# Second layer of a two-layer MLP kernel: block products by seven in a fourth group, sums by accumulating transfers, and x blocks placed earlier

## The chip, the cores and the metric

The kernel runs on one core of one Trainium2 chip. The metric is the time of one execution on the device in microseconds (us). The core's engines are called as in the profile: PE multiplies matrices, PEld loads its weights, DVE and ACT work on vectors, POOL is the general engine, and SP issues most of the DMAs. PE reads SBUF and writes sums to PSUM; DVE and ACT carry them from there to SBUF.

## The reference

An attention without softmax gives x (4608 tokens, 512 columns), and two layers follow. All data are float32.

```python
kv = np.einsum('bhsd,bhse->bhde', k, v)
out = np.einsum('bhsd,bhde->bhse', q, kv)          # then scaled by its rms and g_norm
# layer 1:  h = x @ w_in;  g = relu(h) ** 2;   x = g @ w_out      (w_in 512 x 2048, w_out 2048 x 512)
# layer 2:  h = x @ w_in;  g = h * cos(h);   out = g @ w_out
```

## The kernel before

**Products in three parts.** Each float32 operand is split into a high part in PE's reduced float32 format (a copy on ACT, names ending in `h`) and a low part (a subtraction on DVE, names ending in `l`). A product is three matmuls: high by high, high by low, low by high.

**The stages.** The attention and one half of layer 1's hidden units run first, in 72 chunks (`run_chunks`, to about 501 us). While they run, the weights are converted: `load_w` and `conv_steps` read a piece of raw weights, split it and store it in DRAM, as `wi_d` (first products), `ws_d` (second products by seven) or `wo_d` (plain second products). Items of the kind "seven" cost four more DVE differences, and more ACT and DVE splitting, than items of the kind "out". After that come 30 slots (`run_slots`): 10 for the rest of layer 1 (five tiles of tokens with two groups of hidden units each), and 20 for layer 2 (five tiles with four groups). Four tiles have 1024 tokens and the last one has 512. In this text a slot is named by its number from 0 to 29; slots 10 to 13 are the four groups of layer 2's first tile, and 26 to 29 those of its last tile.

**A slot.** The first product (`first_product`, line 502) is done as a product of 2 x 2 blocks with seven block products instead of eight (the Winograd form), which is 84 matmuls. Its two PSUM tiles FA and FB take turns, and between the block products ACT and DVE read them (`keep`, `add`, `last`). Then the activation runs, in layer 2 the five steps `cos_1` to `cos_5` for each of four blocks, three on ACT and two on DVE. The second product of the slot follows 1.25 slots after its first product (`LAG2`), and its matmuls are interleaved with the first product of the next slot. It has two forms. In the set `seven` (line 82) it is done by seven block products as well (`second_product`, line 675): `s_block` makes four differences on DVE and seven splits (ACT and DVE), and in layer 2 a full tile takes 168 matmuls of 256 columns. Each of the seven sums is carried by `drain_product` from PSUM (tiles SA and SB, in turn) into one of four running sums in SBUF, by a DVE addition (line 698), or by an ACT copy (line 695) where the running sum begins. Groups that are not in `seven` go the plain way (`second`, line 604, then `drain`): four splits (`g_hi`, `g_lo`), 96 matmuls of 512 columns in a full tile, and eight DVE additions of half size (line 624).

**Order and queues.** Each step has a place in units of a slot, given with `at(pos(...))`; `PH` is a seventh of a slot. Instructions of one engine run in order. SP issues the weight loads `wi` (line 476), `ws` (481) and `wo` (486) of 512 KB each, the loads of a tile's x (`load_quads`, line 442), and the results (`later`, line 842): the DMA of a result waits on SP until its last addition has been made, and the loads behind it wait as well. Weights and running sums share 16 buffers (`w_p`), the x blocks 13 (`x`), and the activation's tiles 18 (`c`). `x_block` (lines 452, 470, 471) makes the seven blocks of a tile's x, 11 DVE instructions and 7 on ACT, at -1.9 to 4.1 sevenths of a slot from the tile's first slot; `load_quads` stands at -3.6 and -2.6 sevenths.

Of the kernel before, what the change touches and what calls it, by code (L numbers as in the profile page):

```python
# [8 lines left out]
F32 = mybir.dt.float32  # L9
# [7 lines left out]
P = 128  # L17
# [5 lines left out]
def kernel(  # L23
# [55 lines left out]
    wi_d = {  # L79
        (m, q): dram.tile([P, NPR, 2, 2, 2, P], F32, name=f"wi_d{m}_{q}") for m in range(2) for q in groups_of[m]  # L80
    }
    seven = {(0, 0)} | {(1, q) for q in range(NP - 1)}
    ws_d = {k: dram.tile([P, NPR, 2, 2, 2, P], F32, name=f"ws_d{k[0]}_{k[1]}") for k in sorted(seven)}
    wo_d = {
        (m, f): dram.tile([P, 2, DM], F32, name=f"wo_d{m}_{f}")
# [338 lines left out]
    W_OF = (0, 1, 3, 4, 6, 5, 2)  # L424
    BLOCKS = {(0, 0): 2, (1, 1): 5, (0, 1): 6, (1, 0): 7}
    S_ORDER = (0, 2, 3, 4, 5, 1, 6)
    xb, wi, wo, kept, hs, ys, sums, quads = {}, {}, {}, {}, {}, {}, {}, {}

    def big(pool, dtype, name, ht):
# [157 lines left out]
    def second(k, n):  # L587
        m, t, q = slots[k]
        ht = TILES[t][1]
        todo = units(k)[4 * n:4 * n + 4]  # L590
        for a, c in enumerate(CHUNKS):
            pp, u = divmod(c, 2)
            w = wo[k, c]
            for b, (j, i) in enumerate(todo):
                ps = psum["SA" if b < 2 else "SB"][:, b % 2, :512 if m else ht]
                g = gs[k, (u, j)]
                cs = slice(i * P, (i + 1) * P)
                for x, y in ((0, 0), (0, 1), (1, 0)):
                    if m == 0:
                        lhs, rhs = w[:, x, cs], g[y][:, pp, :]  # L600
                    else:
                        lhs, rhs = g[y][:, pp, cs], w[:, x, :]
                    last = a == 3 and (x, y) == (1, 0)
                    nc.tensor.matmul(  # L604
                        ps, lhs, rhs, start=(a == 0 and (x, y) == (0, 0)), stop=last, skip_group_check=True
                    )
                    if last and b % 2:
                        drain(k, 2 * n + b // 2)
                    yield

    def drain(k, n):
        m, t, q = slots[k]
        t0, ht = TILES[t]
        j, i = units(k)[2 * n]
        ps = psum[("SA", "SB")[n % 2]]
        if m == 0:
            e, ps = sums[m, t, i // 2, j][:, :, :ht], ps[:, :, :ht]
            nc.vector.tensor_tensor(out=e, in0=ps, in1=e, op=ALU.add)
            if q == groups_of[m][-1]:
                later(0.1, nc.sync.dma_start, out=y_d[t][:, j, i:i + 2, :], in_=e)  # L620
            return
        for d in range(2):
            e = blocks_of(t, sums[m, t, d, j])[:, i:i + 2, :]
            nc.vector.tensor_tensor(out=e, in0=ps[:, :, 2 * P * d:2 * P * (d + 1)], in1=e, op=ALU.add)
            if i + 2 == ht // P:
                dst = out[t0 + j * ht:t0 + (j + 1) * ht, 2 * P * d:2 * P * (d + 1)]
                later(0.1, nc.sync.dma_start, out=dst.rearrange("(b p) n -> p b n", p=P), in_=blocks_of(t, sums[m, t, d, j]))

    def s_block(k, i):
        m, t, q = slots[k]  # L630
# [23 lines left out]
    def blocks_of(t, x, m=1):  # L654
        if m == 0:
            return x[:, :, :TILES[t][1]]
        return x.rearrange("p c n -> p (c n)").rearrange("p (b n) -> p b n", n=2 * P)[:, :TILES[t][1] // P]
# [32 lines left out]
    def drain_product(k, i):  # L690
        m, t, q = slots[k]
        ps, (d, j) = blocks_of(t, s_bank(k, i), m), SUM_OF[i]
        if q == 0 and m and i in (0, 2, 3, 6):
            sums[m, t, d, j] = e = w_p.tile([P, 2, 512], F32, tag="w", name="sum")
            nc.scalar.copy(out=blocks_of(t, e), in_=ps)
        else:
            e = blocks_of(t, sums[m, t, d, j], m)
            nc.vector.tensor_tensor(out=e, in0=ps, in1=e, op=ALU.add)


    chunks = [(t, f) for t in range(NTILE) for f in range(NH)]
# [5 lines left out]
    def at(n, fn, *a):  # L707
        jobs.append((n, len(jobs), fn, a))
# [25 lines left out]
    def outs_of(m, ps):  # L734
        return [("out", m, f, 1) for p in ps for f in (2 * p, 2 * p + 1)]

    def pairs_in(m, ps, kind="pair"):
        return [(kind, m, p, i) for p in ps for i in range(2)]
# [4 lines left out]
        w_items += new  # L743
        w_at += [n + step * k for k in range(len(new))]
    for new, n0, n1 in (
        (pairs_in(0, range(4, 6), "seven") + outs_of(0, range(6, 8)) + outs_of(1, range(6, 8)) + pairs_in(1, range(4), "seven"), 13, nAtt + 1),
        (pairs_in(0, range(NP, 2 * NP)), nAtt + 1, nA0 - 6),
        (pairs_in(1, range(2 * NP)) + pairs_in(1, range(4, 6), "seven"), pos(0.5), pos(9)),
    ):
        w_items += new  # L750
        w_at += [n0 + (n1 - n0) / len(new) * k for k in range(len(new))]
# [24 lines left out]


    PH = 1 / 7
    for k, (m, t, q) in enumerate(slots):
        if q == 0:  # L780
            for a in range(2):
                at(pos(k + (a - 3.6) * PH) if k else nA0 - 6, load_quads, m, t, a)
            for f, i in enumerate(ORDER):
                at(pos(k + (f - 1.9) * PH) if k or f > 2 else nA0 - 4 + f, x_block, k, i)
        for f, i in enumerate(ORDER):
            at(pos(k + (f - 2.7) * PH) if k or f > 2 else nA0 - 5 + f / 2, load_wi, k, i)
        if (m, q) in seven:
# [48 lines left out]
    def later(delay, fn, **a):  # L836
        pending.append((here + delay, fn, a))
# [118 lines left out]
```

## Time and profile before

| what | us |
|---|---|
| median of 3 runs (lowest, highest) | 1594.78 (1592.71, 1594.97) |
| the profiled execution, its own time | 1593.87 |
| its span in the trace | 1592.1 |
| PE busy | 1555.1 |
| DVE busy | 1273.3 |
| ACT busy | 992.7 |

The granted clock of PE over the span is 0.994 of full speed. 1.8 us of the execution's time lie outside the span. In the rows further down, times in a window or in a timeline are us from the span's start. A row of the windows view lists for a stretch each engine's busy time with the number of its instructions, then the granted clock, the mean busy share of the 16 DMA engines and the rate.

### The profile page before, as it was taken

What the parts mean: (1) busy time and instruction counts of PE and PEld (TensorE: products, weight loads), DVE (VectorE), ACT (ScalarE), POOL (GpSimd) and SP (SyncE); (2) the same over time, 40 slices, a digit from 0 to 9 for tenths busy, and PEclk for the clock granted to TensorE, in tenths of its full rate; (3) what the DMA queues carried; (4) which work ended last, traced back from release to release, by engine and by line L of the source; (5) the groups of instructions that cost most, each with busy time, mean ns of one, the idle gap of its engine ahead of it and who ended that gap; (6) DMA issues with size and microseconds to landing.
All of it is one profiled execution on the core that took longest, in us unless ns stands there. A gap on an engine that the chain in (4) does not pass through costs nothing.

```text
span 1592.1 us, 23679 instructions
## 1 busy us (share of the span) xinstructions
PE 1555.1 (98%) x8840; PEld 1322.0 (83%) x8840; DVE 1273.3 (80%) x1724; ACT 992.7 (62%) x1422; POOL 60.8 (4%) x58
## 2 busy tenths in 40 slices
PE   5999999999999999999999999999999999999998
PEld 4777777778887778888888899889988998899897
DVE  7967767787766898989867789868986898689786
ACT  5977767784434666556646666666666666666664
POOL 1100112111100000000000000000000000000000
PEclk8999999999999999999999999999999999999999
DMA  9855876665568989898988856565656565656684
GB/s 316 279 168 159 256 238 223 200 207 184 164 214 274 318 283 352 304 353 292 351 311 333 286 177 212 180 244 172 212 187 237 172 213 180 229 174 206 214 338 191
DMA packets 214545, 382.20 MB, mean 240 GB/s; under 512 B 17312, under 2 KB 140704, under 8 KB 214432
## 3 DMA queue, kind: packets, MB, share of 16 engines
q1 hardware_dynamic: 213664, 378.34, 71.0%
q0 software_dynamic: 768, 2.36, 0.4%
q8 instruction: 70, 1.15, 0.3%
q14 instruction: 43, 0.35, 0.1%
HBM read 301.99 MB, written 78.64 MB: 239 GB/s over the span
## 4 chain that ended last, share of the span: by engine, by line
PE 87%; DVE 6%; DMA 3%; ACT 3%; issue 1%; SPq 0%; POOL 0%; DVEq 0%; ACTq 0%
PE FA L502 15%; PE FB L502 15%; PE SA L675 11%; PE SB L675 10%; PE acc L415 10%; PE l L378 8%; PE SA L604 6%; PE SB L604 6%; PE o L378 1%; PE ss L378 1%; DMA q<-in_qT 1%; PE o L257 1%; DMA x_d<-xo 1%; PE l L257 0%; DVE raw L173 0%
## 5 line engine op out<-in xcount | busy, mean ns | idle before, releaser
L502 PE MATMUL FA<-xh,wi 128*128 128x512 f32 (+1 forms) x840 | 304.0, 371 | 4.7 <-DVE h L526 1.7
L502 PE MATMUL FB<-xh,wi 128*128 128x512 f32 (+1 forms) x840 | 301.7, 369 | 0.0
L675 PE MATMUL SA<-ws,gh 128*128 128x256 f32 x792 | 197.0, 280 | 0.0
L675 PE MATMUL SB<-ws,gh 128*128 128x256 f32 x720 | 180.1, 280 | 0.0
L502 PEld LDWEIGHTS FA<-xh,wi 128*128 128x128 f32 x840 | 158.3, 189 | 20.8 <-DVE h L526 2.1
L502 PEld LDWEIGHTS FB<-xh,wi 128*128 128x128 f32 x840 | 157.7, 188 | 13.5
L675 PEld LDWEIGHTS SA<-ws,gh 128*128 128x128 f32 x792 | 147.8, 188 | 14.6 <-issue 0.2
L675 PEld LDWEIGHTS SB<-ws,gh 128*128 128x128 f32 x720 | 134.8, 188 | 13.6
L561 DVE SCALAR_TENSOR_TENSOR y<-y,h 128x1024 f32<-128x1024 f32 (+1 forms) x80 | 89.2, 1115 | 46.7 <-ACT y L557 46.7
L543 ACT ACTIVATE y<-h,zerob 128x1024 int32<-128x1024 f32 (+1 forms) x80 | 85.1, 1063 | 64.9 <-DVE h L522 64.9
L553 ACT ACTIVATE y<-y 128x1024 f32<-128x1024 f32 (+1 forms) x80 | 78.0, 976 | 75.8 <-DVE y L547 75.3
L415 PE MATMUL acc<-gh,wh 128*128 128x512 f32 x288 | 114.3, 398 | 0.0
L415 PE MATMUL acc<-gl,wh 128*128 128x512 f32 x288 | 113.5, 394 | 0.0
L415 PE MATMUL acc<-gh,wl 128*128 128x512 f32 x288 | 113.1, 393 | 0.0
L675 PE MATMUL SA<-ws,gl 128*128 128x256 f32 x396 | 111.0, 280 | 0.0
L502 PE MATMUL FB<-xl,wi 128*128 128x512 f32 (+1 forms) x300 | 110.9, 370 | 0.0
L502 PE MATMUL FA<-xl,wi 128*128 128x512 f32 (+1 forms) x300 | 110.8, 369 | 0.0
L652 DVE TENSOR_TENSOR gl<-y,gh 128x1024 fp32r<-128x1024 f32 (+1 forms) x75 | 83.5, 1114 | 30.0 <-ACT gh L651 30.0
L675 PE MATMUL SB<-ws,gl 128*128 128x256 f32 x360 | 100.9, 280 | 0.0
L378 PE MATMUL l<-xh,wh 128*128 128x512 f32 x240 | 96.5, 402 | 1.7 <-ACT xh L347 0.8
L378 PE MATMUL l<-xl,wh 128*128 128x512 f32 x240 | 94.9, 396 | 0.0
L378 PE MATMUL l<-xh,wl 128*128 128x512 f32 x240 | 94.4, 393 | 0.0
(190 smaller groups left out, 3859.8 us busy)
## 6 DMA issues: line engine op xcount, KB each, us to landing
wi<-wi_d SPq DMA_DIRECT2D x210, 512.0 KB, 5.1
ws<-ws_d SPq DMA_DIRECT2D x140, 512.0 KB, 5.3
wo<-wo_d SPq DMA_DIRECT2D x40, 512.0 KB, 5.2
kvld<-in_kv SPq DMA_DIRECT2D x32, 512.0 KB, 6.3
wi_d<-wh SPq DMA_DIRECT2D x24, 448.0 KB, 3.5
wi_d<-raw SPq DMA_DIRECT2D x24, 448.0 KB, 3.8
raw<-in_wA SPq DMA_DIRECT2D x20, 512.0 KB, 6.0
q<-in_qT SPq DMA_DIRECT2D x32, 288.0 KB, 4.0
```

The costliest lines, as they stand in the source:

```text
L257: nc.tensor.matmul(kv_ps[b][r, p, r], t[:n, 0, head], t[:n, 1, head], start=(c == 0 and p == 0), stop=(c == NSC - 1), skip_group_check=True,)
L378: nc.tensor.matmul(ps, a[:, 0, cs], m[:], start=(c == 0 and k == 0), stop=(c == NKC - 1 and k == 2))
L415: nc.tensor.matmul(o, a[:, cs], m[:], start=(f == 0 and n == 0), stop=(f == NH - 1 and n == 2), skip_group_check=True)
L502: nc.tensor.matmul(ps[:, pp, :], a, b, start=(i in (0, 1, 2) and n == 0), stop=(n == 5), skip_group_check=True)
L543: nc.scalar.activation(out=y.bitcast(I32), in_=hs[k, b], func=AF.Identity, bias=zerob)
L553: nc.scalar.activation(out=y, in_=y, func=AF.Sin, scale=math.pi)
L561: nc.vector.scalar_tensor_tensor(out=y, in0=y, scalar=-2.0 * math.pi, in1=hs.pop((k, b)), op0=ALU.add, op1=ALU.mult)
L604: nc.tensor.matmul(ps, lhs, rhs, start=(a == 0 and (x, y) == (0, 0)), stop=last, skip_group_check=True)
L652: nc.vector.tensor_tensor(out=l, in0=src, in1=as32(h), op=ALU.subtract)
L675: nc.tensor.matmul(ps[:, b, :], lhs, rhs, start=(i in (0, 1, 2) and n == 0 and (m == 0 or b % 2 == 0)), stop=(n == 5), skip_group_check=True,)
```

## The change

Layer 2's fourth group is added to `seven`, so that all four groups of a tile have their second products by seven. Four of the seven sums (block products 4, 5, 1 and 6, the last four in the order) are no longer added by DVE, except at the start of a running sum and in the very last slot: ACT copies them from PSUM to one of two `raw` buffers, and a DMA that POOL issues adds them to the running sum in SBUF. The four results of a tile are stored one after the other behind these four sums, a quarter of a slot later. The conversion of four plain pieces of layer 2's second weights ("out") is replaced by four pieces of the kind "seven", at the same place in the list. The x blocks of a tile are placed at -4.5 to 3.5 sevenths of a slot instead of -1.9 to 4.1, and their loads at -6.8 and -5.8 instead of -3.6 and -2.6. That holds for the tiles of both layers.

```diff
-    seven = {(0, 0)} | {(1, q) for q in range(NP - 1)}
+    seven = {(0, 0)} | {(1, q) for q in range(NP)}
...
+    BY_DMA = (4, 5, 1, 6)
...
-                ps = psum["SA" if b < 2 else "SB"][:, b % 2, :512 if m else ht]
+                ps = psum["SA" if b < 2 else "SB"][:, b % 2, :ht]
...
             e = blocks_of(t, sums[m, t, d, j], m)
-            nc.vector.tensor_tensor(out=e, in0=ps, in1=e, op=ALU.add)
+            if m and i in BY_DMA and k < len(slots) - 1:
+                part = blocks_of(t, conv_p.tile([P, 2, 512], F32, tag="raw", name="part"))
+                nc.scalar.copy(out=part, in_=ps)
+                nc.gpsimd.dma_start(out=e, in_=part, accum_op=ALU.add)
+            else:
+                nc.vector.tensor_tensor(out=e, in0=ps, in1=e, op=ALU.add)
+        if m and q == groups_of[m][-1] and i in (4, 5, 1, 6):
+            t0, ht = TILES[t]
+            dst = out[t0 + j * ht:t0 + (j + 1) * ht, 2 * P * d:2 * P * (d + 1)]
+            last_one = k == len(slots) - 1
+            later(0 if last_one else 0.25, nc.sync.dma_start, out=dst.rearrange("(b p) n -> p b n", p=P), in_=e)
...
-        (pairs_in(0, range(4, 6), "seven") + outs_of(0, range(6, 8)) + outs_of(1, range(6, 8)) + pairs_in(1, range(4), "seven"), 13, nAtt + 1),
+        (pairs_in(0, range(4, 6), "seven") + outs_of(0, range(6, 8)) + pairs_in(1, range(6, 8), "seven") + pairs_in(1, range(4), "seven"), 13, nAtt + 1),
...
+    X_AT = (-4.5, -3.5, -1.9, -0.7, 0.6, 2.0, 3.5)
     for k, (m, t, q) in enumerate(slots):
         if q == 0:
             for a in range(2):
-                at(pos(k + (a - 3.6) * PH) if k else nA0 - 6, load_quads, m, t, a)
+                at(pos(k + (a - 6.8) * PH) if k else nA0 - 6, load_quads, m, t, a)
             for f, i in enumerate(ORDER):
-                at(pos(k + (f - 1.9) * PH) if k or f > 2 else nA0 - 4 + f, x_block, k, i)
+                at(pos(k + X_AT[f] * PH) if k or f > 2 else nA0 - 4 + f, x_block, k, i)
```

The part of `drain` that belonged to layer 2's plain form is removed.

## Rows read from the trace of the kernel before

**Rows 1.** The page, part 1: busy us, share of the span, instructions.

```profile
PE 1555.1 (98%) x8840; PEld 1322.0 (83%) x8840; DVE 1273.3 (80%) x1724; ACT 992.7 (62%) x1422; POOL 60.8 (4%) x58
```

**Rows 2.** Waits of PE from 862 to 1592 us: total, times, longest.

```profile
PE SA L604 <- ACT y L557: 0.8, 1, 0.8
```

**Rows 3.** Timeline of PE: start, us, instruction; a 512-column and a 256-column stretch.

```profile
598.65 0.39 PE L502 MATMUL FA<-xh,wi 128*128 128x512 f32 x1
...
602.28 0.39 PE L604 MATMUL SB<-gl,wo 128*128 128x512 f32 x1
...
1572.23 0.28 PE L675 MATMUL SB<-ws,gh 128*128 128x256 f32 x1
...
1574.98 0.28 PE L675 MATMUL SA<-ws,gh 128*128 128x256 f32 x1
```

**Rows 4.** Windows view: slots 16 and 17, a tile's third and fourth group.

```profile
1082.10:1121.30 39.20, 39.20 (x254) 35.58 (x253) 32.62 (x29) 24.17 (x25) 0.00 (x0) 1.00 0.59 188
1121.30:1160.50 39.20, 39.20 (x254) 35.57 (x253) 37.08 (x34) 26.90 (x28) 0.00 (x0) 1.00 0.67 215
```

**Rows 5.** Groups of DVE, 1075 to 1160 us: busy us, mean ns, idle before.

```profile
L698 DVE TENSOR_TENSOR sum<-SB,sum 128x1024 f32<-128x1024 f32 x8 | 9.8, 1220 | 1.3 <-PE SB L675 1.3
```

**Rows 6.** Groups of ACT, 1075 to 1160 us, with the same columns.

```profile
L695 ACT COPY sum<-SA 128x1024 f32<-128x1024 f32 x1 | 1.0, 1012 | 0.0
```

**Rows 7.** Line 354, the kernel's only DMAs issued by POOL (144 KB each).

```profile
L354 POOL DMA_DIRECT2D x_d<-xo x16: 539/539/764, 26.7 to 83.6; - x16
...
DMA to landing us min/median/max: 2.0/5.3/7.6
```

**Rows 8.** Line 476, the loads wi (512 KB): 1080 to 1120, then 1519 to 1560.

```profile
DMA to landing us min/median/max: 4.3/4.6/4.7
...
DMA to landing us min/median/max: 6.5/8.2/9.9
```

**Rows 9.** Windows view: three stretches in which the DMA engines are full.

```profile
838.00:858.00 20.00, 16.65 (x123) 15.59 (x123) 16.70 (x24) 12.54 (x22) 0.00 (x0) 0.95 1.02 379
856.10:859.50 3.40, 3.40 (x11) 2.62 (x10) 3.40 (x4) 1.04 (x1) 0.00 (x0) 0.50 1.04 424
...
1519.00:1569.00 50.00, 50.00 (x419) 50.00 (x419) 41.81 (x67) 34.40 (x61) 0.00 (x0) 1.00 1.01 400
```

**Rows 10.** Timeline of SP where the fourth tile's results leave.

```profile
1507.76 0.32 SPq L476 DMA_DIRECT2D wi<-wi_d  x1
1518.07 0.99 SPq L842 DMA_DIRECT2D out<-sum  x2
```

**Rows 11.** Timeline of PE at the start of slot 10.

```profile
851.50 0.28 PE L675 MATMUL SB<-gh,ws 128*128 128x256 f32 x1
853.34 0.49 PE L502 MATMUL FA<-xh,wi 128*128 128x512 f32 x1 [1.56 <-ACT xh L470]
855.62 0.50 PE L502 MATMUL FA<-xraw,wi 128*128 128x512 f32 x1 [1.79 <-DVE xraw L471]
```

**Rows 12.** Timeline of SP before slot 10 (which begins at 853 us).

```profile
827.76 0.42 SPq L476 DMA_DIRECT2D wi<-wi_d  x1
834.97 2.22 SPq L842 DMA_DIRECT2D y_d<-sum  x2
...
839.27 2.00 SPq L442 DMA_DIRECT2D xraw<-y_d  x2
```

**Rows 13.** Timeline of PE at the end: the last slot's second product.

```profile
1576.10 0.47 PE L604 MATMUL SA<-wo,gh 128*128 128x512 f32 x1 [0.83 <-ACT y L557]
...
1586.89 0.39 PE L604 MATMUL SB<-wo,gh 128*128 128x512 f32 x1
```

**Rows 14.** Timeline of DVE at the end.

```profile
1576.51 0.68 DVE L561 SCALAR_TENSOR_TENSOR y<-y,h 128x512 f32<-128x512 f32 x1
...
1587.31 1.29 DVE L624 TENSOR_TENSOR sum<-SB,sum 128x512 f32<-128x512 f32 x2
```

**Rows 15.** Groups of the whole span, with the columns of rows 5.

```profile
L173 DVE TENSOR_TENSOR raw<-raw 128x128 f32<-128x128 f32 x160 | 43.5, 313 | 1.5
```

More of the change, by code (lines that the diff above doesn't have):

```diff
@@ L620, in drain @@
                 later(0.1, nc.sync.dma_start, out=y_d[t][:, j, i:i + 2, :], in_=e)
[L621 to L627, printed above, removed]
     def s_block(k, i):
```

## The prediction

> **What bounds the kernel now.** I read the page's busy times first: PE is busy 98% of the span, DVE 80%, ACT 62% [rows 1]. A busy PE can still be a stalled one, so the list of PE's own waits came next. From 862 us to the end, which is nearly all of layer 2, it has a single entry of 0.8 us [rows 2]. There the time is the number of matmuls times their spacing and nothing else. The timeline gives the spacing: 16 steps of 512 columns take 602.28 - 598.65 = 3.63 us, 0.227 us each, and 23 steps of 256 columns take 2.75 us, 0.120 us each [rows 3]. A check: a slot with 84 matmuls of 512 and 168 of 256 columns should take 19.1 + 20.2 = 39.2 us, and slots 16 and 17 do take 39.20 [rows 4]. So in layer 2 whatever removes PE time is gained in full, as long as the other engines and the transfers stay in time. Three places are not of this kind: the start of slot 10, the loads around the last tile, and the end.
>
> **Part 1, the fourth group by seven.** In a full tile 96 matmuls of 512 columns (96 x 0.227 = 21.8 us) become 168 of 256 (168 x 0.120 = 20.2 us), which saves 1.6 us a tile and 6.4 us in four tiles. The columns fall by an eighth, but the smaller matmul takes 0.120, more than half of 0.227 (0.1135), so two fifths of that eighth are lost to spacing. The last tile has half: 48 x 0.227 = 10.9 becomes 84 x 0.120 = 10.1, so 0.8 us; I count it with the end.
>
> **Part 2, vector work.** What hides this is DVE's and ACT's slack. In a full tile DVE has now, in instructions of full size, 44 of activation and first-product sums, 33 + 4 of splits and differences, 17 sums, 8 half sums and 11 of x blocks, so 109 and 8 halves. Afterwards it has 44 + 44 + 9 + 11 = 108, since 15 of a tile's sums leave for the DMA. One costs about 1.1 us (37.08/34 in slot 17 [rows 4]; the single one is 1.22 long and overlaps the next [rows 5]). That is 119 us of the tile's 157, 76%. Slot 17, where x blocks, splits and seven sums meet, is at 37.08 of 39.20 today and PE does not wait [rows 2, 4]; four fewer sums stand there afterwards. ACT gets up to four copies of 1.01 us a slot [rows 6] and, in the slot after a fourth group, three more splits: slot 17's 26.90 us [rows 4] become about 31 of 39.2, 79%. I cost both at nothing. If the cover is gone, a copy that is late by more than one block product's time (39.2/7 = 5.6 us) less its own 1.0 holds PE, because the next product but one uses the same PSUM tile.
>
> **Part 3, the accumulating transfers.** About 70 DMAs of 512 KB (256 KB in the last tile) are new, and no such transfer is in the trace. Two things wait for them. ACT's third copy needs the buffer of the first, two products later, and DVE's sum of product 0 in the next slot needs the running sum that product 1 added to, also two products later. So the time from ACT's copy to the landing is free up to about 11.2 - 1.0 = 10 us in full tiles and about 5 us in the last. Bounds: POOL's DMAs of 144 KB landed in 2.0 to 7.6 us [rows 7], SP's loads of 512 KB in 4.3 to 9.9 us [rows 8]. I take 6 to 8 us, nearest to the loads of equal size in a stretch that is not full, plus the second read. That costs nothing in the full tiles, where the DMA engines are busy for 0.59 to 0.67 of a slot [rows 4] and four more transfers of 1.3 us (512 KB at the 400 GB/s of the full stretch [rows 9]) add 0.13. The Trainium skill ("DMA: Bandwidth & Descriptors", section "Anatomy of one DMA — SWDGE (gpsimd) path") gives about 2.0 us plus the bytes at 436 GB/s for such a DMA, an estimate of 3.2 us here; the loads of 512 KB in this trace took 4.3 at least, and by either price the full tiles have nothing to pay.
>
> **Part 4, the last tile.** Here the transfers are short of time. SP waits from 1507.76 to 1518.07 for the previous tile's last sum, with loads queued behind [rows 10]. From 1519 to 1569 the DMA engines are full at 1.01 and 400 GB/s [rows 9], and loads land 8.2 us after issue instead of 4.6 [rows 8]. PE gets through without a wait [rows 2], by a margin that these rows don't give. The change lengthens SP's wait: the last result now waits for a copy and a transfer (7 to 9 us) instead of two half sums, though it stands 0.15 slot (about 3 us) further back. It adds three 512 KB weight loads for the last slot (3.9 us) and some eight accumulations of 256 KB at 0.66 us (5 us) to the full stretch. The bounds are nothing, if the margin takes it all, and the sum of what is added, about 9 us. I take 1.5, nearer the lower end, since the last slot has no first products behind it whose weights would have to come too.
>
> **Part 5, x blocks sooner.** Slot 10 begins with two waits of PE, for ACT's and for DVE's first x block, 1.56 and 1.79 us [rows 11]. Then 3.4 us pass at half clock, at 1.2 GHz in place of 2.4, after the engine had stood twice [rows 9], which costs half of that, 1.7 us. In all 1.6 + 1.8 + 1.7, some 5 us. The cause stands in SP's queue: the x loads are issued at 839.27, behind a store that SP could issue only at 834.97, while nothing had been issued since 827.76 [rows 12]. Slot 9 has half a tile, 156 matmuls of 256 columns and 23 of 512, so 18.7 + 5.2 = 23.9 us by their spacing [rows 3]. The loads move forward by 3.2 sevenths of it, 10.9 us, which puts them ahead of that wait, and the blocks by 2.6 sevenths, 8.9 us. So the wait should go. But the DMA engines are full there (1.02 from 838 to 858 [rows 9]), and four x loads (4 x 1.3 = 5.2 us) now go ahead of weights that PE needs as well: something else may be late by up to 5 us. Between a gain of 5 and a loss of about 1, I take a gain of 3.5. In the other tiles the earlier x blocks only spread DVE's work; I cost them at nothing, from -1.5 to +3 over the four tile changes in layer 1, where the weight conversion fills DVE too.
>
> **Part 6, the end.** PE waits 0.83 us before the last slot's plain product [rows 13]. By seven, the second of the block products needs a difference with the block that the activation's last step finishes at 1576.51 + 0.68 [rows 14]; difference, high copy and low part follow, near 0.7 us each, so to 1579.2 if nothing moves. PE ends the slot before at 1575.1 [rows 3] and its first product (12 x 0.120) at 1576.5. It could come earlier, as DVE has fewer sums then: a wait of 0 to 2.7, I take 1.3. At the end one sum follows the last matmul, not two of 0.6 each [rows 14]. So -0.8 (columns) - 0.6 + 1.3 - 0.8 = -0.9, from -2.2 to +0.6.
>
> **Part 7, conversion.** Each of the four pieces has four more differences (4 x 0.31 us [rows 15]) and a subtraction of 896 columns (about 1.1 by the 1.22 of 1024 columns [rows 5]) on DVE, so 10 us in all, spread over the chunks. DVE is idle for a fifth of the span [rows 1], and I cost it at nothing, up to +1.
>
> **Sum.** Against the profiled execution of 1593.87: -6.4 + 0 + 0 + 1.5 - 3.5 - 0.9 + 0 = -9.3, so 1584.6. This execution is 0.9 below the median of three runs, inside their spread of 2.3; I add half and say 1585.
>
> **The rivals.**
> *A, the accumulating transfers land too late* (slower). If one takes more than about 10 us from copy to landing, ACT stands before its third copy and DVE before product 0's sum, once a slot in 15 slots of full tiles, and sooner in the last tile. At 12 us that is some 2 us a slot, 30 us, so about 1615. It turns the gain into a loss from a wait of about 0.6 us a slot, a landing near 10.6 us. For it: 9.9 us for a load in the full stretch, and an operation that the trace lacks. Against it: 4.3 to 4.7 in the ordinary slots [rows 8].
> *B, the last tile becomes bound by transfers.* If an accumulation costs the DMA engines two reads, eight of them take 10.5 us instead of 5, and with three loads 14 us are added to a stretch that is already full; PE's margin and the shorter last slot take perhaps 5, so 9 us of waiting in place of 1.5, and about 1592.5, no change. The Trainium skill says as much in "Collectives: The Full Stack", section "The bandwidth ceiling: the fold count and why AG ≠ RS ≠ AR": an add pushes two source reads through the same read ring and runs at half the rate of a copy. No run here shows it yet.
> *C, the x blocks gain nothing.* The wait at slot 10 stays or moves to a weight load: 1588.5, still faster.
>
> **How the numbers follow.** The forecast has 0.54 (1579 to 1589), C 0.15, B 0.14, A 0.17. The low end is with all 5 us of slot 10 and no wait in the last tile, 1593.87 - 6.4 - 5 - 2.2 = 1580, less 1.5 for the tile changes: 1578. The high end takes in B with 4 us for the bounds of the parts costed at nothing: 1596. Outside are most of A and a little below. A difference of 0.2% (3.2 us) is about what a measurement here tells from no change. Faster by more is the forecast and C with a small share lost, 0.68; within it B, 0.14; slower A and some of B, 0.18.
>
> **What would show it.** Right: a full tile of layer 2 takes 1.6 us less; no 1.56 and 1.79 in front of slot 10 and no half clock; POOL's DMAs land under 10 us. Wrong: rows of PE waiting for DVE's line of sums or for ACT's copy in every slot (A); PE waiting for wi or ws after 1500 us and DMA shares of 1.0 throughout the last tile (B); the same waits at slot 10 (C).

## The result and the profile after

The changed kernel takes 1611.41 us (median of 5 runs, 1609.54 to 1613.46), the kernel before 1594.78 beside it. The ratio is 1.0105, with a 95% interval of 1.0093 to 1.0117: slower by 1%, 16.6 us, where 9.3 less were forecast.

The profiled execution took 1609.54 us, its span is 1607.7. From the page of the kernel after: the busy times (part 1), the queue of the DMAs that POOL issues (part 3: packets, MB, share of 16 engines) and its new transfers (part 6: KB each, median us to landing).

```profile
PE 1557.3 (97%) x9164; PEld 1335.5 (83%) x9164; DVE 1254.3 (78%) x1711; ACT 1062.2 (66%) x1512; POOL 117.4 (7%) x125
...
q0 software_dynamic: 10992, 36.71, 11.3%
...
sum<-part POOLq DMA_DIRECT2D x60, 512.0 KB, 7.5
```

Beside [rows 1], DVE has lost 19 us and ACT has gained 69.5, while PE is busy for as long as before: the shares say little. Where the time went is seen when both spans are cut at the same slots. Windows view of the kernel before (columns as in [rows 4]): slots 0 to 2; slots 9 and 10; slots 11 to 25; slot 26 to the end.

```profile
501.50:599.30 97.80, 93.77 (x409) 76.54 (x410) 78.64 (x103) 60.39 (x65) 0.00 (x0) 1.00 0.92 302
827.60:886.40 58.80, 55.45 (x349) 49.87 (x348) 42.55 (x48) 32.52 (x43) 0.00 (x0) 0.97 0.85 312
886.40:1477.40 591.00, 591.00 (x3548) 526.22 (x3547) 491.75 (x440) 380.12 (x379) 0.00 (x0) 1.00 0.62 205
1477.40:1592.10 114.70, 109.04 (x775) 102.21 (x773) 83.67 (x125) 63.88 (x105) 0.00 (x0) 0.99 0.67 252
```

The same stretches of the kernel after:

```profile
506.60:610.10 103.50, 96.03 (x409) 77.55 (x410) 78.14 (x101) 60.13 (x64) 0.00 (x0) 0.98 0.87 288
838.50:895.20 56.70, 54.44 (x349) 48.94 (x348) 41.23 (x48) 32.28 (x43) 0.00 (x0) 1.00 0.87 318
895.20:1481.20 586.00, 586.00 (x3764) 531.55 (x3763) 468.83 (x406) 431.43 (x441) 45.15 (x53) 1.00 0.88 262
1481.20:1607.70 126.50, 111.26 (x883) 108.07 (x881) 86.09 (x121) 79.65 (x129) 15.31 (x18) 0.98 0.94 306
```

| stretch | before | after | difference |
|---|---|---|---|
| the chunks, up to slot 0 | 501.5 | 506.6 | +5.1 |
| slots 0 to 2 | 97.8 | 103.5 | +5.7 |
| slots 3 to 8 | 228.3 | 228.4 | +0.1 |
| slots 9 and 10 | 58.8 | 56.7 | -2.1 |
| slots 11 to 25 | 591.0 | 586.0 | -5.0 |
| slot 26 to the end | 114.7 | 126.5 | +11.8 |
| the span | 1592.1 | 1607.7 | +15.6 |

So there are three losses, each in a stretch of its own. The full tiles brought what was meant (three of the four lie in slots 11 to 25; the fourth tile's last product runs in slot 26). DMA engines are busy for 0.88 of the full tiles, up from 0.62, and for 0.94 of the last.

PE's waits in the kernel after, the largest (total, times, longest), in slots 0 to 2; from 895 to 1481 us the same view has no entry:

```profile
PE FA L503 <- DVE h L527: 2.8, 1, 2.8
PE FA L503 <- ACT m L517: 1.9, 1, 1.9
```

The same from slot 26 to the end:

```profile
PE SA L669 <- ACT part L694: 2.4, 2, 1.7
PE SA L669 <- issue: 2.0, 1, 2.0
PE SB L669 <- ACT part L694: 1.6, 1, 1.6
PE FB L503 <- DMA wi<-wi_d: 1.6, 2, 0.8
PE FA L503 <- DMA wi<-wi_d: 1.2, 2, 0.8
```

L503 is the first product in the changed kernel, L669 the second by seven, L694 ACT's copy of a sum for the transfer, L695 the transfer, L697 DVE's sum, L477 the load wi. "Issue" stands for a wait for which the profile names nothing.

### The profile page after: what moved, and what is told of

It is laid out like the page before. It is cut to its first block, busy times and chain, and to the rows that moved or that the text cites. A ratio compares the mean times of both kernels' runs of the same rounds, so it can differ in the third digit from the quotient of the medians.

```text
span 1607.7 us, 24781 instructions
## 1 busy us (share of the span) xinstructions
PE 1557.3 (97%) x9164; PEld 1335.5 (83%) x9164; DVE 1254.3 (78%) x1711; ACT 1062.2 (66%) x1512; POOL 117.4 (7%) x125
## 3 DMA queue, kind: packets, MB, share of 16 engines
q0 software_dynamic: 10992, 36.71, 11.3%
## 4 chain that ended last, share of the span: by engine, by line
PE 80%; DMA 8%; DVE 6%; ACT 2%; issue 2%; SPq 1%; POOL 0%; DVEq 0%; ACTq 0%; POOLq 0%
PE FB L503 14%; PE FA L503 14%; PE SA L669 12%; PE SB L669 11%; PE acc L415 10%; PE l L378 9%; PE SA L605 3%; PE SB L605 3%; DMA wi<-wi_d 1%; DMA sum<-part 1%; DMA x_d<-xo 1%; PE o L378 1%; PE ss L378 1%; DMA wi_d<-raw 1%; DMA q<-in_qT 1%
## 5 line engine op out<-in xcount | busy, mean ns | idle before, releaser
L503 PE MATMUL FA<-xh,wi 128*128 128x512 f32 (+1 forms) x840 | 304.3, 372 | 7.7 <-DVE h L527 2.8
L503 PE MATMUL FB<-xh,wi 128*128 128x512 f32 (+1 forms) x840 | 303.4, 371 | 3.9 <-DMA wi<-wi_d 2.9
L669 PE MATMUL SA<-ws,gh 128*128 128x256 f32 x1008 | 250.3, 282 | 4.4 <-ACT part L694 2.4
L669 PE MATMUL SB<-ws,gh 128*128 128x256 f32 x1008 | 249.1, 281 | 3.2 <-ACT part L694 1.6
L669 PEld LDWEIGHTS SA<-ws,gh 128*128 128x128 f32 x1008 | 188.0, 189 | 23.1 <-ACT part L694 2.8
L669 PEld LDWEIGHTS SB<-ws,gh 128*128 128x128 f32 x1008 | 187.2, 188 | 21.7 <-ACT part L694 1.8
L503 PEld LDWEIGHTS FA<-xh,wi 128*128 128x128 f32 x840 | 158.5, 190 | 20.2 <-issue 4.0
L503 PEld LDWEIGHTS FB<-xh,wi 128*128 128x128 f32 x840 | 158.3, 189 | 15.2 <-DVE xraw L453 1.5
L695 POOL DMA_DIRECT2D sum<-part x71 | 60.5, 852 | 1120.2 <-ACT part L694 1090.5
L669 PE MATMUL SA<-ws,gl 128*128 128x256 f32 x504 | 141.9, 281 | 0.3 <-DVE gl L646 0.2
L669 PE MATMUL SB<-ws,gl 128*128 128x256 f32 x504 | 141.5, 281 | 0.2 <-DVE gl L646 0.2
L415 PE MATMUL acc<-gh,wh 128*128 128x512 f32 x288 | 114.5, 399 | 0.0
L415 PE MATMUL acc<-gl,wh 128*128 128x512 f32 x288 | 113.7, 395 | 0.0
L503 PE MATMUL FB<-xl,wi 128*128 128x512 f32 (+1 forms) x300 | 111.2, 371 | 0.0
L503 PE MATMUL FA<-xl,wi 128*128 128x512 f32 (+1 forms) x300 | 110.9, 370 | 0.0
L669 PEld LDWEIGHTS SA<-ws,gl 128*128 128x128 f32 x504 | 95.3, 189 | 9.7 <-DVE gl L646 0.7
L669 PEld LDWEIGHTS SB<-ws,gl 128*128 128x128 f32 x504 | 94.9, 188 | 9.3 <-DVE gl L646 0.4
L548 DVE SCALAR_TENSOR_TENSOR y<-y,h 128x1024 f32<-128x1024 int32 (+1 forms) x80 | 89.0, 1112 | 12.5 <-ACT y L544 12.5
```

The lines of the kernel that those rows point to most:

```text
L415: nc.tensor.matmul(o, a[:, cs], m[:], start=(f == 0 and n == 0), stop=(f == NH - 1 and n == 2), skip_group_check=True)
L503: nc.tensor.matmul(ps[:, pp, :], a, b, start=(i in (0, 1, 2) and n == 0), stop=(n == 5), skip_group_check=True)
L548: nc.vector.scalar_tensor_tensor(out=y, in0=y.bitcast(I32), scalar=-1.0, in1=hs[k, b], op0=ALU.mult, op1=ALU.add)
L669: nc.tensor.matmul(ps[:, b, :], lhs, rhs, start=(i in (0, 1, 2) and n == 0 and (m == 0 or b % 2 == 0)), stop=(n == 5), skip_group_check=True,)
L695: nc.gpsimd.dma_start(out=e, in_=part, accum_op=ALU.add)
```

## The experiments

The theory after the result: the three losses are independent. (1) The longer conversion costs PE time in the chunks. (2) The earlier x blocks of layer 1's first two tiles stand ahead of what PE needs on DVE and ACT. (3) Each accumulating transfer keeps the DMA engines busy for two transfers, and in the last tile there is no room. The rivals: a shortage of vector time, ACT's two buffers, or one cause behind all three. Edits are against the changed kernel where nothing else is said. The runs were made in several sets, each with the kernel before beside it; its median was between 1593.0 and 1594.8 us, and a ratio is against the kernel before of the same set. So a difference between medians of different sets is sure to some 2 us, and the length of a stretch comes from one profiled execution of each kernel.

### The conversion alone

The kernel before, with its list of conversions changed. Its fourth group then has no plain weights of its own and reads layer 1's, in loads of the same size:

```
-        ... outs_of(0, range(6, 8)) + outs_of(1, range(6, 8)) + pairs_in(1, range(4), "seven"), 13, nAtt + 1),
+        ... outs_of(0, range(6, 8)) + pairs_in(1, range(6, 8), "seven") + pairs_in(1, range(4), "seven"), 13, nAtt + 1),
```

> The kernel before, with only the converted pieces swapped as in the change (the fourth group's plain product reads layer 1's stored weights instead of its own, so that everything that is timed stays). My theory: the longer conversion costs the 3.5 us that chunks 29 to 33 lost, so 1598. The rival: the start of the chunks varies from run to run by as much, and the conversion costs nothing: 1594 to 1596. A third: it also delays slots 0 to 2, so about 1603.

1598.41 us (7 runs), ratio 1.0034 (1.0021 to 1.0048): 4.9 slower. Slot 0 begins 5.7 us late (507.2 against 501.5); from there to the end it takes 1092.0 us, 1.4 more than the kernel before. The place of the loss is one stretch of the chunks. ACT's timeline in this kernel:

```profile
267.65 0.51 ACT L186 CAST wh<-raw 128x384 fp32r<-128x384 f32 x1 [3.13 <-DVE raw L169]
268.19 0.37 ACT L271 COPY kvx<-o 64x256 f32<-64x256 f32 x1
```

PE's, at the same place:

```profile
268.61 0.45 PE L292 MATMUL o<-q,kvx 64*64 64x288 f32 x1 [1.86 <-ACT kvx L271]
```

The windows around it:

```profile
240.80:279.50 38.70, 36.35 (x231) 28.08 (x228) 26.91 (x58) 26.46 (x60) 5.23 (x4) 0.96 0.72 206
269.80:273.20 3.40, 3.40 (x9) 2.65 (x8) 2.19 (x6) 3.40 (x10) 0.00 (x0) 0.50 0.91 246
```

ACT waits 3.13 us for DVE before it can split a piece of the weights. Behind that wait on ACT stands a copy of the attention (L271) which PE needs, and PE stands for 1.86 us. Then 3.4 us pass at a granted clock of 0.50, 1.2 GHz. The stretch is 38.7 us long; in the kernel before it is 33.6 with no wait. DVE is busy for 26.9 of the 38.7, so it isn't short of time: an instruction at the wrong place in a queue is enough. In the changed kernel the same stretch (242.0 to 279.0 us) takes 37.0, with waits of 1.5 and 0.8 for ACT and no half clock; 1.9 of its 5.1 arise in the first 50 us already, before the swapped pieces, where the traces of all these kernels differ by up to 2.6 us. So the +5.1 is partly chance. In the ten traces with the swapped pieces in the chunks slot 0 begins at 501.7 to 507.2 us. That the pieces cost something is seen at two fixed matmuls of the chunks, which stand at 255.9 and 290.1 us in the kernel before: they are 34.2 to 34.3 us apart in the three kernels without these pieces there and 35.3 to 39.8 in the ten with them.

### The x blocks at their old places

```
-    X_AT = (-4.5, -3.5, -1.9, -0.7, 0.6, 2.0, 3.5)
+    X_AT = (-1.9, -0.9, 0.1, 1.1, 2.1, 3.1, 4.1)
...
-                at(pos(k + (a - 6.8) * PH) if k else nA0 - 6, load_quads, m, t, a)
+                at(pos(k + (a - 3.6) * PH) if k else nA0 - 6, load_quads, m, t, a)
```

> The changed kernel with the x blocks and x loads at the places of before. My theory: the earlier x blocks and loads are what costs slots 0 to 2 (about 6 us more than before, up to 599/610 us) and what saves slot 10's wait (it lasts 30.0 us in place of 33.1). Undoing them gives some 6 us back in slots 0 to 2 and loses 3 to 5 at slots 9 and 10: 1608 to 1611, with slot 3 beginning at about 604. The rival: slots 0 to 2 lose because the whole queue order shifted with the converted weights; then they stay as slow as now and the time is 1614 to 1616.

1613.34 us (4 runs), ratio 1.0138 (1.0108 to 1.0168), between the theory's 1611 and the rival's 1614. Slots 0 to 2 are back at 97.6 us. But the fourth group of three tiles (slots 13, 17, 21) now takes 41.0, 41.3 and 41.6 us in place of 39.2, and slot 10 is late again. PE's waits of this kernel in the full tiles:

```profile
PE SA L669 <- issue: 5.2, 3, 2.1
```

Each of the three ends 0.1 us behind a DVE sum, and that sum stands in DVE's queue behind an x block. Ahead of the first:

```profile
982.03 1.22 DVE L453 TENSOR_TENSOR xraw<-xraw 128x1024 f32<-128x1024 f32 x1 [3.47 <-DMA xraw<-y_d]
```

The x load lands too late there, which it doesn't in the kernel before, with the same places and no transfers. So the change needs the early places in layer 2, and loses by them in layer 1. The next kernel takes them apart.

### The old places only for the first two tiles

```
+                at(pos(k + (a - (6.8 if k >= 4 else 3.6)) * PH) if k else nA0 - 6, load_quads, m, t, a)
...
+                at(pos(k + (X_AT[f] if k >= 4 else f - 1.9) * PH) if k or f > 2 else nA0 - 4 + f, x_block, k, i)
```

> The changed kernel with one edit: the tiles at slots 0 and 2 keep the places of x blocks and x loads of before, all later tiles have the earlier ones. Theory (about 6 us of the loss are due to the x blocks of these two tiles, and the gain at slot 10 is independent of it): slots 0 to 2 take 97 to 98 us in place of 103.6, slots 9 and 10 stay at 56.7 together, the last tile stays at about 126, and the time is 1604 to 1606. Rival (DVE's arrears of slots 0 to 2 only move to a later slot): slots 3 to 10 together grow by as much as slots 0 to 2 lose, and the time stays at 1610 or more.

1604.89 us (4 runs), ratio 1.0077 (1.0063 to 1.0091): 6.5 us less than the changed kernel (4.5 by the ratios). Windows of slots 0 to 2 and of slots 9 and 10:

```profile
506.70:604.10 97.40, 93.86 (x410) 76.59 (x411) 77.04 (x99) 59.70 (x64) 0.00 (x0) 1.00 0.91 300
832.80:891.20 58.40, 55.77 (x350) 50.46 (x349) 41.42 (x48) 32.26 (x43) 0.00 (x0) 0.97 0.84 312
```

The loss of slots 0 to 2 is these two tiles' alone and doesn't come back later (slots 3 to 8 take 228.7). Over all thirteen traces slots 0 to 2 take 97.0 to 97.8 us with the old places of these tiles and 101.2 to 106.0 with the early ones. Slots 9 and 10 miss the expectation by 1.7; the kernel with four buffers (below), which has the changed kernel's places, takes 58.2 there as well, so this may be the spread of executions. How such a loss looks, in the changed kernel: DVE has no gap here, and two of the five rows ahead of `h` (L527) are x blocks (L472, L453); PE waits for that `h`. Then it runs at a granted clock of 0.51 (1.2 GHz) for 3.4 us, as the window of 568.2 to 571.6 us shows. DVE's timeline:

```profile
562.70 1.22 DVE L472 TENSOR_TENSOR xl<-xt,xh 128x1024 fp32r<-128x1024 f32 x1
...
565.77 1.22 DVE L453 TENSOR_TENSOR xraw<-xraw 128x1024 f32<-128x1024 f32 x1
566.91 1.22 DVE L527 TENSOR_TENSOR h<-FA,u 128x1024 f32<-128x1024 f32 x1
```

PE's timeline, then the window:

```profile
568.19 0.77 PE L503 MATMUL FA<-xh,wi 128*128 128x512 f32 x1 [2.79 <-DVE h L527]
```

```profile
568.20:571.60 3.40, 3.40 (x8) 2.72 (x9) 3.40 (x4) 3.34 (x4) 0.00 (x0) 0.51 0.59 189
```

### All sums on DVE

```
-    BY_DMA = (4, 5, 1, 6)
+    BY_DMA = ()
```

> The changed kernel with no accumulating transfers: all sums added by DVE. My theory: the last tile loses about 12 us because of them (they land in 7 us where 5 are free, ACT waits for its buffer, and the DMA engines are full), and DVE can take the sums in the full tiles with at most short waits; so 1600 to 1605. The rival: DVE is what the transfers relieve; then PE waits for DVE in every full tile, 3 us or more a tile, and the time stays at 1611 or above.

1595.99 us (10 runs), ratio 1.0017 (1.0004 to 1.0031): 15.4 us less than the changed kernel (14.0 by the ratios), from this one edit, and below the 1600 to 1605 expected. Windows of slots 11 to 25 and of slot 26 to the end:

```profile
892.50:1478.60 586.10, 586.10 (x3765) 531.62 (x3764) 522.74 (x459) 386.10 (x387) 0.00 (x0) 1.00 0.67 214
1478.60:1592.30 113.70, 107.22 (x883) 106.01 (x881) 100.33 (x140) 69.15 (x112) 0.00 (x0) 0.99 0.76 282
```

DVE is busy for 89% of the full tiles (522.7 of 586.1) and PE doesn't wait: the transfers relieve an engine that had no need of it. The last tile falls from 126.5 to 113.7 us. Of these 12.8 us, 0.4 lie in slot 26, 5.6 in slots 27 and 28, and 6.8 in the last slot (47.4 against 40.6). Other traces with the same code in the last tile have 126.3 and 128.4 with the transfers, and 113.5, 115.8 and 116.0 without, so the difference is 10 to 15 us.

### The last tile's sums on DVE, then those of the group before it too

```
-            if m and i in BY_DMA and k < len(slots) - 1:
+            if m and i in BY_DMA and t < len(TILES) - 1:
```

> The changed kernel with accumulating transfers in the four full tiles alone; the last tile's sums are DVE's. My theory: slots 26 to 29 and the end, 126 us now and 115 before, fall to about 116, so 1600 to 1602. The rival: the last tile is slow through the three more weight loads and the later results alone, and the transfers do not matter: 1608 to 1611.

1602.43 us (4 runs), ratio 1.0053 (1.0035 to 1.007): 9.0 less than the changed kernel (8.3 by the ratios). Slot 26 to the end takes 117.0. The second kernel has `k < len(slots) - 5` there:

> The changed kernel, but the four products' sums are added by DVE in the last five slots' groups (slots 25 to 29), not by accumulating transfers: beyond e4_last_tile_by_dve, where slots 26 to 29 are so, the last full tile's fourth group too, whose results SP stores early in the last tile. Theory (what e4 still has over e3_all_sums_by_dve in the last tile, 117.0 against 113.7 us from the start of slot 26 to the end, comes from SP standing before these results, which wait for a copy and a transfer each, with the last tile's loads behind them): the stretch takes 113.5 to 114.5 us, and the time is about 1599, 3 less than e4's 1602.4. Rival (it is noise of the last slots or the accumulations of earlier groups): the stretch stays at 116 to 118 and the time at 1602.

1598.95 us (10 runs), ratio 1.0034 (1.0022 to 1.0046): 3.5 less again (3.0 by the ratios), as the theory had it, but the two intervals overlap, so the times alone don't settle it. Slot 26 to the end takes 114.5 in its profiled execution (1589.67 us, the shortest of the ten; slot 0 begins at 501.7 in it). Slots 27 and 28 take 22.7 and 20.2 us, as in every trace without transfers, where the kernel with the last tile's sums alone on DVE has 24.6 and 20.6. SP shows what is gained. Its last issues of the fourth tile's results, in the changed kernel (three of four) and then in this one (two of four); x2 takes in two results and the wait between them:

```profile
1518.61 6.25 SPq L848 DMA_DIRECT2D out<-sum  x2
...
1528.17 0.39 SPq L848 DMA_DIRECT2D out<-sum  x1
```

```profile
1508.94 4.71 SPq L848 DMA_DIRECT2D out<-sum  x2
```

Slot 26 begins 7.8 us later in the one than in the other; the last result leaves about 15 us later (1528.2 against some 1513.3). Measured from the slot's start, SP is held for 7 us longer, and the loads of the last tile stand behind it. With the last tile's sums alone on DVE SP is held as long as in the changed kernel (47.3 and 47.0 us from the slot's start, against 39.8). So of the 12.8 us between 126.5 and 113.7, by these traces, 9.5 go to the last tile's own accumulations and 2.5 to 3 to the group before it.

### The same transfers without the addition

```
-                nc.gpsimd.dma_start(out=e, in_=part, accum_op=ALU.add)
+                nc.gpsimd.dma_start(out=e, in_=part)
```

> The changed kernel with the transfers' addition left out: POOL's DMAs copy the part over the running sum. Same number, bytes written, queue and waits. My theory: the addition reads twice, so a copy takes the DMA engines about half (POOL's queue has 11.3% of the DMA engines now, it would be about 6%), lands in 5 us in place of 7.5, and most of the last tile's loss goes: 1602 to 1605. The rival: the landing is set by POOL's way of issuing and not by the second read; then 7 us, 11% and 1611 stay.

1600.45 us (10 runs), ratio 1.0042 (1.0031 to 1.0054). From its page, the queue and the transfers:

```profile
q0 software_dynamic: 10288, 36.71, 5.7%
...
sum<-part POOLq DMA_DIRECT2D x60, 512.0 KB, 6.1
```

The window of slots 11 to 25:

```profile
895.00:1481.00 586.00, 586.00 (x3773) 532.05 (x3772) 468.75 (x407) 430.81 (x441) 28.68 (x54) 1.00 0.78 261
```

The bytes are the same (36.71 MB), the share of the DMA engines is half. Without POOL's older DMAs (0.4% of the span before, 6.4 us), 11.3% of 1607.7 less 6.4 is 175 us for the equal of 65.5 transfers of 512 KB, 2.7 us each; 5.7% of 1594.9 less 6.4 is 84.5, 1.3 each. So an accumulation costs 2.1 copies. With copies the last tile takes 117.1 us (1477.8 to 1594.9): the addition alone is worth 11.0 us of the whole (10.0 by the ratios).

### Four buffers in the last tile

```
-                part = blocks_of(t, conv_p.tile([P, 2, 512], F32, tag="raw", name="part"))
+                part = (
+                    blocks_of(t, conv_p.tile([P, 2, 512], F32, tag="raw", name="part"))
+                    if t < len(TILES) - 1
+                    else temp([P, 512], F32, "part").rearrange("p (b n) -> p b n", n=2 * P)
+                )
```

> The changed kernel, with four buffers in place of two for the accumulating transfers of the last tile. My theory: of the 9.5 us that these transfers cost in the last tile, about half is ACT's wait for a buffer (2.9, 1.7 and 1.7 us at the places where PE stands behind ACT's copies), and the other half is weights that land late because the DMA engines are full: 1605 to 1608. If the buffers were all: 1602. If the DMA engines were all: 1611, with the same waits for wi and ws.

1610.15 us (4 runs), ratio 1.0102 (1.0077 to 1.0127): nothing gained, where 1605 to 1608 were expected. ACT's waits for a buffer, in the changed kernel (two buffers) and in this one (four), and after them two of PE's waits of this one:

```profile
ACT part L694 <- DMA sum<-part: 8.5, 5, 2.9
```

```profile
ACT part L698 <- DMA sum<-part: 2.2, 2, 1.7
```

```profile
PE SB L669 <- issue: 4.8, 1, 4.8
PE SB L669 <- ACT sum L689: 2.2, 1, 2.2
```

ACT's wait goes and PE's comes back under other names. The longest, of 4.8 us, ends at 1595.46, right behind a DVE sum that had waited for a transfer to land:

```profile
1594.67 0.69 DVE L701 TENSOR_TENSOR sum<-SB,sum 128x512 f32<-128x512 f32 x1 [4.35 <-DMA sum<-part]
```

With more buffers ACT no longer stands, but the running sum isn't ready any sooner. Buffers aren't the cause; the transfers behind them are.

### Versions without the losses

With the sums on DVE and the early places in layer 2 alone (`X_AT[f] if m else f - 1.9`, and the loads likewise):

> The changed kernel with all sums by DVE, and the earlier x blocks and x loads in layer 2's tiles alone (layer 1 at the places of before). My theory: the earlier x blocks cost 6 us in slots 0 to 2 (103.6 us against 97.8 before) and save 2 at slots 9 and 10; this keeps the saving without the cost. Slots 0 to 2 return to 97 to 99 us, slot 10 stays at 30.0, the time is 1589 to 1591, some 6 us below the kernel with all sums by DVE and below the kernel before. The rival: slots 0 to 2 depend on the queue order that the conversion leaves, and stay at 102 or more: 1595.

1592.99 us (10 runs), ratio 0.9988 (0.9973 to 1.0002): above the 1589 to 1591 expected, and not told apart from the kernel before. Slots 0 to 2 take 97.0, but slot 9 grows to 29.3 us, with new waits of PE for ACT (1.1 and 2.2), and the gain of slots 9 and 10 is gone (58.8). Next, the four pieces of the conversion moved out of the chunks:

```
-  ... outs_of(0, range(6, 8)) + pairs_in(1, range(6, 8), "seven") + pairs_in(1, range(4), "seven"), 13, nAtt + 1),
+  ... outs_of(0, range(6, 8)) + pairs_in(1, range(4), "seven"), 13, nAtt + 1),
...
+        (pairs_in(1, range(6, 8), "seven"), pos(10.5), pos(13)),
```

> As the kernel with DVE sums and earlier x blocks in layer 2 alone, and the fourth group's four weight pieces are converted in slots 10.5 to 13 and not in the chunks. My theory: chunks 28 to 36 lose 2 to 5 us through the longer pieces, and layer 2's first tile has room on DVE and DMA, so 1586 to 1588. The rival: DVE is at 82% there and the pieces only move the wait: PE waits in slots 11 to 13 and the time is 1590 or more.

1588.37 us (8 runs), ratio 0.997 (0.9955 to 0.9984): faster than both kernels. Slot 0 begins at 496.3, 5 us before that of the kernel before: a stall at 196 us that the kernel before has as well (PE waits 3.7 us for DVE's `m`, L328, and runs at half clock after it) doesn't come with the items further apart. Last, with the early places from slot 4 on:

> The version of e6_conversion_later (all sums on DVE, four pieces converted in slots 10 to 12), with the earlier places of the x blocks also for layer 1's last three tiles; only the tiles at slots 0 and 2 keep the places of before. Theory (the earlier x blocks cost time only in slots 0 to 2, where the conversion fills DVE and ACT; further on they are free, and the late start of slot 10 in e6 comes from slot 9 having its own x blocks late): slots 0 to 2 stay at 97 us, slots 9 and 10 together fall from 61.4 to about 57, and the time is 1584 to 1586. Rival (the order of layer 1's x blocks doesn't matter there; slot 9 is late because DVE and ACT take up the conversion): slots 9 and 10 stay above 60 us and the time stays at 1588.

1586.03 us (6 runs), ratio 0.9957 (0.9944 to 0.997), the best of all. Its windows of slots 0 to 2, 9 and 10, and 26 to the end, then PE's longest wait:

```profile
496.50:593.60 97.10, 93.84 (x409) 76.49 (x410) 76.98 (x99) 59.69 (x64) 0.00 (x0) 1.00 0.92 300
823.60:884.60 61.00, 56.03 (x349) 50.48 (x348) 45.50 (x58) 33.92 (x45) 0.00 (x0) 0.97 0.84 318
1471.40:1584.90 113.50, 107.22 (x883) 106.02 (x881) 100.37 (x140) 69.14 (x112) 0.00 (x0) 0.99 0.77 283
```

```profile
PE SB L669 <- DVE sum L697: 4.4, 1, 4.4
```

The time is what was expected (at the upper edge of 1584 to 1586), the reason isn't: slots 9 and 10 stay at 61.0, where the theory had 57, so the rival was right there. DVE has 10 more instructions in them than in the changed kernel (58 against 48). Steps of the conversion (L123 to L187), which the changed kernel doesn't have there, are among them, and PE waits 4.4 us for a sum in this full queue. The intervals of this run and the one before overlap, so what the last edit is worth by itself stays open; both versions are faster than the kernel before, by 0.3 and 0.4%.

## Why the prediction was wrong

Term by term, against the profiled executions:

| part | taken (bounds) | measured | from |
|---|---|---|---|
| 1, full tiles | -6.4 | -6.7 | slots 11 to 25 -5.0; slot 26 31.9 to 30.2 with all sums on DVE |
| 2, vector work | 0 | 0 | no wait of PE from 895 to 1481 us |
| 3, transfers, full tiles | 0 | 0 | the same |
| 4, transfers, last tile | +1.5 (0 to 9) | +12.8 | slot 26 to the end, 126.5 against 113.7 |
| 5, slot 10 | -3.5 (-5 to +1) | -2.1 | slots 9 and 10 |
| 5, layer 1 | 0 (-1.5 to +3) | +5.7 | slots 0 to 2 |
| 6, the end | -0.9 (-2.2 to +0.6) | +0.7 | slot 27 to the end, 82.8 to 83.5 with all sums on DVE |
| 7, conversion | 0 (to +1) | +5.1 | slot 0's start; alone 4.9 |

The measured column adds up to +15.5, the span to +15.6. Each figure is that of one or two traces. By the other traces with the same code in the stretch, Part 4 lies between 10 and 15, slot 10 between -2.4 and -0.5, layer 1 between +3.4 and +8.2, the end between +0.4 and +3.0 and the conversion between +0.2 and +5.7; Part 4 is the largest in any case.

**Parts 1 and 2 held.** A full tile lost 1.6 us, from 40.5 + 39.5 + 39.2 + 39.2 to four times 39.2. DVE stands at 80% of the full tiles (468.8 of 586.0) where 76% was reckoned, which changes nothing: at 89%, with all sums on it, it still held nobody up. That the slack was there also means that the transfers weren't needed, with the x blocks early (all sums on DVE and the old places wasn't run). I costed them, and didn't ask what they were to buy.

**Part 3 held in its result, and its price was half the true one.** The landing was taken at 6 to 8 us and is 7.5 at the median. The view of line L695 of the changed kernel (who waited for it, us and times; the landing), for 900 to 1481 us, then from 1481 us on:

```profile
  DVE sum L697: 1.2, 1
...
DMA to landing us min/median/max: 4.5/7.5/13.1
```

```profile
  ACT part L694: 8.5, 5
  DVE sum L697: 2.7, 1
...
DMA to landing us min/median/max: 3.2/7.4/9.2
```

In the full tiles five of 53 landings went past the free 10 us; DVE waited once, 1.2 us, and PE not at all. So rival A was wrong in the full tiles. This holds with the early x blocks: at the old places, slots 11 to 25 took 592.4 us with the transfers, 6.4 more. But "four more transfers of 1.3 us ... add 0.13" of a slot is the price of copies. Four accumulations of 2.7 us add 0.27 by that reckoning; the share went from 0.67 (all sums on DVE) to 0.88. The Trainium skill's estimate for such a DMA in "DMA: Bandwidth & Descriptors", section "Anatomy of one DMA — SWDGE (gpsimd) path", was 3.2 us: no transfer of 512 KB was as short, 4.5 being the least.

**Part 4 is the step that failed most, at three points.** The first is the count. "Some eight accumulations" are 11 in the last tile (three groups of four, less one where a sum begins), and seven of 512 KB begin in this stretch as well: the last three of slot 24's group and the four of slot 25's, which run in slots 26 and 27. The second is the price: 0.66 us each was taken, and by half of 2.7 it is 1.35. That is 11 x 1.35 + 7 x 2.7 = 34 us of the DMA engines' time, where 5 stood in the sum; the windows give 32 to 33 (0.94 of 126.5 less 0.76 of 113.7). The weight loads were too few as well, three in place of six, since slot 25's group needs three more too, but with all sums on DVE PE doesn't wait for a load here. The third is a step that I had worked out and didn't use: Part 3 gave 5 us from copy to landing as free in the last tile, and 6 to 8 as the landing. The excess went into no term. It is in the trace as PE's waits for `part`, 4.0 us, and as the 2.0 us of "issue": they end at 1574.29, right behind a DVE sum that had waited for a landing:

```profile
1573.49 0.69 DVE L697 TENSOR_TENSOR sum<-SA,sum 128x512 f32<-128x512 f32 x1 [2.69 <-DMA sum<-part]
```

This is rival A's mechanism, and its "sooner in the last tile" came true. The reason for the low value, that the last slot has no loads behind it, was about the wrong transfers. Loads of `wi` in this stretch landed 11.3 us after their issue at the median, against 8.0 with the sums on DVE (line L477, 1512 to 1560 and 1508 to 1552 us):

```profile
DMA to landing us min/median/max: 6.9/11.3/14.4
```

```profile
DMA to landing us min/median/max: 5.3/8.0/10.9
```

Rival B named this mechanism and took it at 9 us of waiting; it is 12.8. Its count was eight, and neither the late landings nor SP's longer stand were in it. The run without the addition shows its core: half the engines' time, and 11 us. The Trainium skill's rule in "Collectives: The Full Stack", section "The bandwidth ceiling: the fold count and why AG ≠ RS ≠ AR", that an add runs at half the rate of a copy, is given for the reduce step of a collective; the 2.1 measured here agree with it. I had given it a chance of 0.14, as if it were a risk; with the engines at 1.01 in [rows 9] it should have had more.

**Part 5 was right at slot 10 and wrong in layer 1.** The two waits of [rows 11] are gone. In their place PE waits twice for `wi`, in slot 9:

```profile
856.27 0.35 PE L503 MATMUL FA<-xh,wi 128*128 128x256 f32 x1 [0.79 <-DMA wi<-wi_d]
...
860.72 0.35 PE L503 MATMUL FB<-xh,wi 128*128 128x256 f32 x1 [1.35 <-DMA wi<-wi_d]
```

That is the "something else may be late" of the text, and 2.1 of the 3.5 is left. Rival C, no gain there, was wrong by that much. In layer 1, "the earlier x blocks only spread DVE's work" was an argument from the busy share. The order decided: an x block that is early stands in front of something that isn't.

**Part 6** had the last slot's wait at 1.3 us. With all sums on DVE it is 0.9 for ACT's high copy and 0.8 for DVE's low part, so near enough; three more of 0.2 to 0.3 for later splits, which had no term, make it 2.3. The total is 0.7 longer instead of 0.9 shorter, just past the bound, and what makes up the rest stays open. Three more traces with the same last tile have 83.2, 85.5 and 85.8; in the two long ones PE runs at a granted clock of 0.50 or 0.51 behind these waits.

**Part 7** costed 10 us of DVE at nothing because DVE is idle for a fifth of the span. The price came from a place in ACT's queue, not from DVE's load: with the conversion alone, 1.9 us of waiting and then 3.4 us at half clock. At 4.9 (3.3 to 7.6 by its interval) it was at least three times the bound of 1.

Of the 24.9 us between the forecast of -9.3 and the +15.6, Part 4 makes 11.3, layer 1's x blocks 5.7, the conversion's stretch 5.1, the end 1.6 and slot 10 1.4; Part 1 gives 0.3 back.

## What to carry to other kernels

Cost an accumulating transfer as two copies, and look for the stretch in which the DMA engines are already full before anything else: there an added transfer is paid for by the loads as well (32 us more of the engines' time cost 12.8 us here). Before work is moved off an engine, ask whether that engine holds anyone up; here, with the x blocks early, it could have taken all of it. A busy share hides nothing by itself: for every instruction that an edit adds or moves, name the one behind it in the same queue and who waits for that, because a stall of 2 to 3 us can be followed by more than 3 us at half clock.

## What the hardware showed that was not expected

- An accumulating DMA from SBUF to SBUF kept the DMA engines busy for 2.7 us per 512 KB, a plain one for 1.3.
- DVE at 89% of 586 us, in order and with PE beside it at every moment, caused no wait.
- After PE had stood (1.9 us in the chunks, 2.8 ahead of slot 2), its granted clock was 0.50 or 0.51 for 3.4 us, 1.2 GHz in place of 2.4, as at slot 10 of the kernel before [rows 9]. The 1.9 us in slot 0 of the changed kernel were not followed by it. With the early places in layer 2 alone it was 0.51 for 6.8 us in the last slot, where PE had waited 0.9 and 0.8 us.
- Moving four pieces of the conversion out of the chunks freed a stall far from them, at 196 us, which the kernel before has too: slot 0 begins at 496.3 and 496.5 us in the two traces, against 501.5.
